# Output chunks of the second layer follow their slices by 2.1 slots instead of 2.2

## The chip, the cores and the metric

The kernel runs on one core of one Trainium2 chip. The metric is the device time of one launch in microseconds (us), median of three runs: 1363.01 before the change (1361.18 to 1366.76). TensorE (PE in the profile) multiplies, VectorE (DVE) and ScalarE (ACT) work on tiles element by element, GpSimd (POOL) does some subtractions and issues the loads of weights, SyncE (SP) issues the other transfers. Each engine works through its own list in order, and waits for the others by semaphores.

## The reference

Attention with 32 landmarks per head gives `x` of 4608 tokens by 512. A first layer without bias follows, `h = ((x @ w1) * (x @ w2)) @ w3 @ w_out`, again 4608 by 512. The second layer, which the change touches, is

```python
def _moe2_ref(x, w_in, w_out):          # x 4608x512, w_in 512x2048, w_out 2048x512
    h = x @ w_in
    g = np.where(h > 0.0, h, np.exp(np.minimum(h, 0.0)) - 1.0)
    return g @ w_out
```

All in float32. The kernel reaches that accuracy by splitting each operand into a high and a low part and adding three products (high by high, high by low, low by high).

## The kernel before

Attention and the first layer take the first 612 us and are not touched. The second layer takes the rest.

**Blocks, slices, slots.** The 4608 tokens are cut into five blocks of 768, 1024, 1024, 1024 and 768 (`BLOCKS`, L31). The 2048 hidden columns are cut into eight slices of 256 (`NPAIR`). One block with one slice is one unit `u`, numbered 0 to 39: block `u // 8`, slice `p = u % 8`. The program goes through 41 *slots*; slot `u` holds the first multiplication of unit `u`, and the later work of the units before it. What stands in a slot, and in which order, is written out by hand in `SLOTS` (L126), by the kind of slot: "narrow" for blocks of 768, "mid" for blocks of 1024, "first" and "last" for the first and the last slice of a block.

**A step** (`h0` to `h6`, `step`, L940) is one of the seven products of a Strassen-like scheme for `x @ w_in`: six matmuls on PE (L925 to L927) into one of four PSUM banks (`hat`, `hmm`). DVE adds each bank to its partners (L956) or ACT copies it (L950); then the bank is free for the step four further on.

**The ELU** of unit `u` begins in slot `u` (`R`, `E`: ACT, L972 to L977) and ends in slot `u + 1` (`s`: DVE L981; `a`: DVE L985 and ACT L990, which gives the high part `eh`; `l`: DVE L996, the low part `el`).

**A chunk** (`oo`, L1015) is the product of 128 tokens of a unit with its 256 rows of `w_out`: six matmuls (L1031 to L1033) that read `eh`, `el` and the weights `wo` of that unit. Chunks of two units share a bank of their own (`oa`): for a pair of units U, U+1 (U even) the list `work` has four rows of chunks, first half of the tokens by U, first half by U+1 (which ends the sums), second half by U, second half by U+1. A row has four chunks in a block of 1024 and three in a block of 768. So a pair has 16 or 12 chunks, called chunk 0, 1, 2, ... here. Each has a due time, and at each `c` in a slot all chunks that are due by then are put in, as one *burst* on PE:

```python
            for k, (a, d) in enumerate(((0, 0), (0, 1), (1, 0), (1, 1))):
                t = u + (FIRST if u + k == 0 else LAG)
                work += [(t + (k * nch + c) / (2 * nch), u + d, a * nch + c) for c in range(nch)]

        def chunks(t):
            n = sum(x[0] <= t + 1e-6 for x in work)
```

A "mid" slot has one burst, after `h6`. A "narrow" and a "first" slot have one after `h3` and one after `h6`.

**What a chunk brings with it.** When a sum is ended, `evict` (L1041) adds the bank to the output tile (DVE, L1009; ACT copies it, L1007, for the first two slices of a block) and stores it. It is called after each step and ahead of each chunk that starts a sum. And the last chunk of a unit issues the load of the weights of the unit two further on into the buffer that it has just read:

```python
            if c == 2 * nch - 1:
                wo2.pop(u)
                if u + 2 < n2 - 2:
                    load_wo(u + 2)
```

There are two such buffers (`wo`, 1 MB a load, L861), and two for the weights of the steps (`wh`, 1.75 MB a load, L852). Both are loaded from POOL's queue, as are POOL's subtractions `tv` for the next block (L891, in the slots of slices 3 to 6). POOL's queue is in order: a load whose buffer is still read holds up what stands behind it. `wh` of unit `u + 1` is issued at the start of slot `u`.

Of the kernel before, what the change touches and what calls it, by code (L numbers as in the profile page):

```python
# [120 lines left out]
"""  # L121


LAG = 2.2
FIRST = 1.9
SLOTS = {  # L126
# [12 lines left out]
def nystrom_moe_kernel(ctx, tc, qT, kT, vm, vr, w12, w3T, w_out1, w_in2, w_out2, out):  # L139
# [490 lines left out]
    with tc.manual_schedule():  # L630
# [419 lines left out]
        for u in range(0, n2, 2):  # L1050
            nch = BLOCKS[units2[u][0]][1] // 256
            for k, (a, d) in enumerate(((0, 0), (0, 1), (1, 0), (1, 1))):
                if u == n2 - 2:
                    a, d = d, a
                t = u + (FIRST if u + k == 0 else LAG)
                work += [(t + (k * nch + c) / (2 * nch), u + d, a * nch + c) for c in range(nch)]
# [112 lines left out]
```

## Time and profile before

| | |
|---|---|
| median of three runs | 1363.01 us |
| the profiled execution's own time | 1363.48 us |
| its span, first to last instruction | 1361.7 us |
| PE busy | 1333.0 us (98%) |
| DVE, ACT, POOL busy | 968.5 (71%), 681.1 (50%), 331.1 us (24%) |
| mean granted clock of PE | 0.998 |

The span is what the profile shows; some 1.8 us of the time lie around it. A matmul's row has a modelled end: matmuls are pipelined, and the next one begins before the row of the one before has ended. So how long PE stood is read from the starts of its rows, and the idle time in brackets is a little less than that. "PEld" is PE's loading of weights into the array, which runs beside the matmuls.

### The profile page before, as it was taken

To read this page: it belongs to the slowest core of one execution; us is meant where nothing else is said; L and a number is where in the kernel's file an instruction comes from. 1 tells how busy PE (TensorE), PEld (TensorE's weight loads), DVE (VectorE), ACT (ScalarE), POOL (GpSimd) and SP (SyncE) were. 2 spreads that over 40 slices of the span, in tenths; PEclk is the share of its full clock that TensorE was granted. 3 is DMA by queue.
4 is the path that set the end of the run, shared out by engine and by line. 5 is a ranking of instruction groups with operands and counts; after the bars stand their busy time and mean duration, and the time that the engine had idled before them with its cause. 6 is when DMAs were issued, how large, how long until landed. Compare 5 with 4: busy or idle time off the path is not lost.

```text
span 1361.7 us, 23607 instructions
## 1 busy us (share of the span) xinstructions
PE 1333.0 (98%) x9504; PEld 1115.1 (82%) x9504; DVE 968.5 (71%) x1628; ACT 681.1 (50%) x1189; POOL 331.1 (24%) x327
## 2 busy tenths in 40 slices
PE   5999999999999999999999999999999999999998
PEld 2458888988888888999988788887888878888897
DVE  7988767776787667447787667975768746786575
ACT  6665444454545354446565444555355454453442
POOL 5544342532562523301200121001110020100000
PEclk9999999999999999999999999999999999999999
DMA  8865436546565343417545544363443633446541
GB/s 344 316 210 175 155 131 220 207 142 214 180 210 181 110 163 119 166 60 293 203 171 182 209 170 170 116 233 116 169 170 120 235 135 128 170 174 239 181 156 46
DMA packets 61326, 241.38 MB, mean 177 GB/s; under 512 B 5409, under 2 KB 14625, under 8 KB 53025
## 3 DMA queue, kind: packets, MB, share of 16 engines
q1 hardware_dynamic: 44576, 124.53, 26.0%
q0 software_dynamic: 16640, 115.35, 23.6%
q8 instruction: 74, 1.21, 0.4%
q14 instruction: 36, 0.29, 0.1%
HBM read 197.92 MB, written 41.94 MB: 176 GB/s over the span
## 4 chain that ended last, share of the span: by engine, by line
PE 91%; DMA 6%; DVE 1%; issue 1%; ACT 0%; POOL 0%; SPq 0%; DVEq 0%; POOLq 0%; ACTq 0%
PE oa L1031 8%; PE oa L1033 8%; PE oa L1032 8%; PE ab L782 6%; PE y L818 5%; PE y L819 5%; PE ab L783 5%; PE y L820 5%; PE ab L784 5%; DMA wo<-wo_d 4%; PE hat L927 4%; PE hat L926 4%; PE hat L925 4%; PE hmm L925 4%; PE hmm L927 4%; PE hmm L926 4%
## 5 line engine op out<-in xcount | busy, mean ns | idle before, releaser
L1031 PE MATMUL oa<-wo,eh 128*128 128x512 f32 x552 | 216.7, 393 | 7.4 <-DMA wo<-wo_d 7.4
L1033 PE MATMUL oa<-wo,el 128*128 128x512 f32 x552 | 216.7, 392 | 0.0
L1032 PE MATMUL oa<-wo,eh 128*128 128x512 f32 x552 | 216.5, 392 | 0.0
L981 DVE SCALAR_TENSOR_TENSOR t<-m,t 128x1024 f32<-128x1024 f32 (+1 forms) x80 | 102.4, 1280 | 106.3 <-ACT m L977 106.2
L972 ACT ACTIVATE m<-g 128x1024 f32<-128x1024 f32 (+1 forms) x80 | 75.7, 968 | 204.4 <-DVE g L956 204.4
L782 PE MATMUL ab<-ath,mh 128*128 128x288 f32 x512 | 157.7, 308 | 1.3 <-DVE g L796 1.2
L861 POOL DMA_DIRECT2D wo<-wo_d x38 | 27.4, 721 | 535.3 <-PE oa L1033 532.6
L818 PE MATMUL y<-gh,w3oh 128*128 128x288 f32 x512 | 156.0, 305 | 0.0
L819 PE MATMUL y<-gl,w3oh 128*128 128x288 f32 x512 | 151.3, 295 | 0.0
L783 PE MATMUL ab<-atl,mh 128*128 128x288 f32 x512 | 151.2, 295 | 0.0
L820 PE MATMUL y<-gh,w3ol 128*128 128x288 f32 x512 | 151.0, 295 | 0.0
L784 PE MATMUL ab<-ath,ml 128*128 128x288 f32 x512 | 150.5, 294 | 0.0
L1031 PEld LDWEIGHTS oa<-wo,eh 128*128 128x128 f32 x552 | 104.0, 188 | 33.1 <-DMA wo<-wo_d 11.5
L990 ACT CAST eh<-t 128x512 fp32r<-128x512 f32 (+1 forms) x160 | 84.3, 574 | 91.0 <-DVE t L985 91.0
L1033 PEld LDWEIGHTS oa<-wo,el 128*128 128x128 f32 x552 | 104.0, 188 | 22.3 <-DVE el L996 0.2
L1032 PEld LDWEIGHTS oa<-wo,eh 128*128 128x128 f32 x552 | 103.9, 188 | 21.7
L782 PEld LDWEIGHTS ab<-ath,mh 128*128 128x128 f32 x512 | 96.0, 188 | 24.8 <-issue 14.3
L818 PEld LDWEIGHTS y<-gh,w3oh 128*128 128x128 f32 x512 | 96.2, 188 | 18.1 <-issue 16.8
L790 ACT COPY a<-ab 128x288 f32<-128x288 f32 x128 | 51.0, 399 | 108.2 <-PE ab L784 107.7
L927 PE MATMUL hat<-yb,wh 128*128 128x512 f32 (+1 forms) x280 | 103.2, 369 | 0.0
L927 PE MATMUL hmm<-yb,wh 128*128 128x512 f32 (+1 forms) x280 | 103.2, 368 | 0.0
L925 PE MATMUL hmm<-yb,wh 128*128 128x512 f32 (+1 forms) x280 | 103.1, 368 | 0.1
(173 smaller groups left out, 3052.5 us busy)
## 6 DMA issues: line engine op xcount, KB each, us to landing
wh<-wh_d POOLq DMA_DIRECT2D x40, 1792.0 KB, 8.9
wo<-wo_d POOLq DMA_DIRECT2D x38, 1024.0 KB, 5.3
wo_raw<-in_w_out_dram SPq DMA_DIRECT2D x24, 512.0 KB, 5.8
q<-in_qT_dram SPq DMA_DIRECT2D x8, 1152.0 KB, 6.5
k<-in_kT_dram SPq DMA_DIRECT2D x8, 1152.0 KB, 6.7
out_dram<-o SPq DMA_DIRECT2D x36, 256.0 KB, 2.3
yd<-ysb SPq DMA_DIRECT2D x15, 576.0 KB, 3.6
w_raw<-in_w3T_dram SPq DMA_DIRECT2D x16, 512.0 KB, 5.8
```

The costliest lines, as they stand in the source:

```text
L782: pe.matmul(p[:, :NH], mh[:, cs], ah[:, blk, :], start=(blk == 0), stop=False)
L783: pe.matmul(p[:, :NH], mh[:, cs], al[:, blk, :], start=False, stop=False)
L784: pe.matmul(p[:, :NH], ml[:, cs], ah[:, blk, :], start=False, stop=(blk == 1))
L818: pe.matmul(a[oc][:, :NH], w3o_hi[fc][:, os_], gh, start=(fc == 0), stop=False)
L819: pe.matmul(a[oc][:, :NH], w3o_hi[fc][:, os_], gl, start=False, stop=False)
L820: pe.matmul(a[oc][:, :NH], w3o_lo[fc][:, os_], gh, start=False, stop=(fc == K1 - 1))
L925: pe.matmul(o, ah, bh[:, kk, :], start=(kk == 0), stop=False)
L926: pe.matmul(o, ah, bl[:, kk, :], start=False, stop=False)
L927: pe.matmul(o, al, bh[:, kk, :], start=False, stop=(kk == 1))
L1031: pe.matmul(oacc[c], eh[:, ts_], w[:, 0, :], start=start and j == 0, stop=False)
L1032: pe.matmul(oacc[c], eh[:, ts_], w[:, 1, :], start=False, stop=False)
L1033: pe.matmul(oacc[c], el[:, ts_], w[:, 0, :], start=False, stop=stop and j == 1)
```

## The change

One number. The due time of a chunk, counted in slots, becomes 0.1 less for all pairs and rows but the very first row, which has its own constant.

```diff
-LAG = 2.2
+LAG = 2.1
```

In the blocks of 1024 the chunks of a pair are due 1/8 slot apart: at U + 2.2, 2.325, ... 3.95, 4.075 before, so the sixteenth (chunk 15) falls into the burst of slot U + 4; at U + 2.1, ... 3.85, 3.975 now, so it falls into the burst of slot U + 3. In the blocks of 768 they are 1/6 slot apart, and the same holds for the twelfth (chunk 11), which was due at U + 4.033 and is now due at U + 3.933. A middle row shifts in the same way: the last chunk of the second row moves from the burst of slot U + 3 to that of slot U + 2.

**PE, end of slot 12** (block 1). `hmm` is the bank of the last step, `wo_9` and `wo_10` the weights of units 9 and 10, the `oa` are the banks of the chunks. Before:

```order
L927 MATMUL hmm_8548<-yb_9610,wh_9985 128x512
L1031 MATMUL oa_10107<-wo_9_9931,eh_9844 128x512
L1032 MATMUL oa_10107<-wo_9_9931,eh_9844 128x512
L1033 MATMUL oa_10107<-wo_9_9931,el_9845 128x512
L1031 MATMUL oa_10107<-wo_9_9931,eh_9872 128x512
L1032 MATMUL oa_10107<-wo_9_9931,eh_9872 128x512
L1033 MATMUL oa_10107<-wo_9_9931,el_9873 128x512
L1031 MATMUL oa_10237<-wo_10_10114,eh_9994 128x512
```

Now the same place:

```order
L925 MATMUL hmm_8548<-yb_9619,wh_9991 128x512
L926 MATMUL hmm_8548<-yb_9620,wh_9991 128x512
L927 MATMUL hmm_8548<-yb_9619,wh_9991 128x512
L1031 MATMUL oa_10237<-wo_10_10114,eh_10000 128x512
L1032 MATMUL oa_10237<-wo_10_10114,eh_10000 128x512
L1033 MATMUL oa_10237<-wo_10_10114,el_10001 128x512
```

The six matmuls of chunk 15 that read `wo_9` now stand seven steps earlier, at the end of slot 11; the burst of slot 12 begins with chunk 0 of the next pair.

**POOL, slots 11 to 13.** Loads and subtractions in the order of the queue; `wo_11` is the load that the chunk shown above issues.

```order
 L861 DMA wo_10_10114<-wo_d 128x2x1024
-L852 DMA wh_10138<-wh_d 128x3584
-L891 TENSOR_TENSOR tv_9988<-yin_9835,tv_9987 128x1024
-L861 DMA wo_11_10234<-wo_d 128x2x1024
-L852 DMA wh_10287<-wh_d 128x3584
-L891 TENSOR_TENSOR tv_9989<-yin_9835 128x1024
+L861 DMA wo_11_10140<-wo_d 128x2x1024
+L852 DMA wh_10146<-wh_d 128x3584
+L891 TENSOR_TENSOR tv_9994<-yin_9843,tv_9993 128x1024
+L852 DMA wh_10293<-wh_d 128x3584
+L891 TENSOR_TENSOR tv_9995<-yin_9843 128x1024
```

The load of the odd unit's weights goes ahead of one load of `wh` and one subtraction; the two loads of `wo` of a pair now stand together.

**DVE, start of a slot in block 1.** L981 is the second `s`, L1009 the evictions, L956 the first sum of the steps. Before:

```order
L981 SCALAR_TENSOR_TENSOR t_10370<-m_10369,t_10370 128x1024
L1009 TENSOR_TENSOR o_10158<-oa_10382,o_10158 128x512
L1009 TENSOR_TENSOR o_10158<-oa_10389,o_10158 128x512
L1009 TENSOR_TENSOR o_10161<-oa_10396,o_10161 128x512
L956 TENSOR_TENSOR s_10463<-hmm_8549,s_10452 128x512
```

Now:

```order
L981 SCALAR_TENSOR_TENSOR t_10377<-m_10376,t_10377 128x1024
L1009 TENSOR_TENSOR o_10166<-oa_10382,o_10166 128x512
L1009 TENSOR_TENSOR o_10166<-oa_10389,o_10166 128x512
L1009 TENSOR_TENSOR o_10169<-oa_10396,o_10169 128x512
L1009 TENSOR_TENSOR o_10169<-oa_10403,o_10169 128x512
L956 TENSOR_TENSOR s_10472<-hmm_8549,s_10460 128x512
```

The fourth eviction of a row, which before stood behind the sums of this slot's last step, now stands with the other three ahead of the first sum.

## Rows read from the trace of the kernel before

**Rows 1.** The page: share of the chain that ended last, by engine.

```profile
PE 91%; DMA 6%; DVE 1%; issue 1%; ACT 0%; POOL 0%; SPq 0%; DVEq 0%; POOLq 0%; ACTq 0%
```

**Rows 2.** Waits of PE and PEld, 612 to 1362 us: total us, times, longest.

```profile
PE oa L1031 <- DMA wo<-wo_d: 7.4, 10, 2.7
...
PEld hmm L925 <- DVE g L956: 0.4, 1, 0.4
PEld oa L1031 <- ACT o L1007: 0.4, 1, 0.4
```

**Rows 3.** Timeline of PE, slots 18 and 19: start, us, instruction, [idle before <- who].

```profile
922.10 0.39 PE L1031 MATMUL oa<-wo,eh 128*128 128x512 f32 x1
...
928.72 0.39 PE L1033 MATMUL oa<-wo,el 128*128 128x512 f32 x1
930.28 0.50 PE L1031 MATMUL oa<-wo,eh 128*128 128x512 f32 x1 [1.17 <-DMA wo<-wo_d]
930.61 0.40 PE L1032 MATMUL oa<-wo,eh 128*128 128x512 f32 x1
...
934.49 0.40 PE L925 MATMUL hat<-yb,wh 128*128 128x512 f32 x1
```

**Rows 4.** Timeline of PE, burst of slot 17: its first matmul, and what follows it.

```profile
901.60 0.39 PE L1031 MATMUL oa<-wo,eh 128*128 128x512 f32 x1
...
912.52 0.40 PE L925 MATMUL hmm<-yb,wh 128*128 128x512 f32 x1
```

**Rows 5.** Timeline of PE, second burst of slot 34.

```profile
1254.20 0.34 PE L927 MATMUL hat<-yb,wh 128*128 128x384 f32 x1
1257.19 0.64 PE L1031 MATMUL oa<-wo,eh 128*128 128x512 f32 x1 [2.65 <-DMA wo<-wo_d]
...
1261.63 0.34 PE L925 MATMUL hat<-yb,wh 128*128 128x384 f32 x1
```

**Rows 6.** Windows around that burst: stretch, us, busy by engine, granted clock, DMA, GB/s.

```profile
1257.00:1258.00 1.00, 0.81 (x2) 0.67 (x3) 0.97 (x2) 0.97 (x2) 0.00 (x0) 0.70 0.87 287
1258.00:1260.00 2.00, 2.00 (x6) 1.56 (x5) 1.46 (x2) 1.97 (x4) 0.00 (x0) 0.50 1.00 416
1260.00:1262.00 2.00, 2.00 (x9) 1.64 (x9) 0.19 (x1) 0.01 (x1) 0.00 (x0) 0.80 0.60 244
```

**Rows 7.** Timeline of POOL: burst of slot 12, and two slots of block 4.

```profile
799.87 0.74 POOL L861 DMA_DIRECT2D wo<-wo_d  x1 [11.33 <-PE oa L1033]
800.61 0.55 POOL L852 DMA_DIRECT2D wh<-wh_d  x1
...
1290.42 0.56 POOL L852 DMA_DIRECT2D wh<-wh_d  x1 [6.51 <-PE hmm L927]
...
1305.97 0.56 POOL L852 DMA_DIRECT2D wh<-wh_d  x1 [2.44 <-PE hat L927]
```

**Rows 8.** The loads of `wo`, and those of `wh`, after 612 us: from issue to landing.

```profile
DMA to landing us min/median/max: 5.2/5.3/9.8
DMA to landing us min/median/max: 7.1/8.9/14.5
```

**Rows 9.** Timeline of DVE and PE: a sum that frees a bank, the matmul that takes it.

```profile
897.18 0.68 DVE L956 TENSOR_TENSOR g<-hat,s 128x512 f32<-128x512 f32 x1
...
900.23 0.39 PE L925 MATMUL hat<-yb,wh 128*128 128x512 f32 x1
...
752.71 0.68 DVE L956 TENSOR_TENSOR g<-hat,s 128x512 f32<-128x512 f32 x1
...
754.56 0.39 PE L925 MATMUL hat<-yb,wh 128*128 128x512 f32 x1
```

**Rows 10.** Timeline of POOL and DVE in the burst of slot 11, and DVE in slot 18.

```profile
786.13 2.41 POOL L891 TENSOR_TENSOR tv<-yin,tv 128x1024 f32<-128x1024 f32 x1
786.20 3.42 DVE L981 SCALAR_TENSOR_TENSOR t<-m,t 128x1024 f32<-128x1024 f32 x1
...
916.17 1.22 DVE L985 TENSOR_TENSOR t<-t,g 128x1024 f32<-128x1024 f32 x1
```

## The prediction

> **What bounds the kernel now.** I read the page's chain first: 91% of it is PE and 6% is DMA [rows 1]. So PE sets the end, and a change of order can only give back time in which PE stands, or make it stand more. The waits of PE in the second layer come next. There is one kind of any weight: chunk matmuls that wait for the load of `wo`, 7.4 us in 10 waits, the longest 2.7 [rows 2]. PEld's waits for other engines are two of 0.4 us [rows 2]. The third view is PE's timeline at those waits. All ten stand in even slots: 10, 12, 14, 18, 20, 22, 26, 28, 30 in the blocks of 1024, and 34 in the last block. In slot 18 the burst begins at 922.10, and at 928.72 + 0.23, after five chunks, PE stops until 930.28 [rows 3]. The sixth chunk (chunk 4 of the new pair) is the first of the odd unit and needs that unit's weights. POOL's timeline says why they are late: in slot 12 the load is issued at 799.87, right when chunk 15 of the pair before has been done, since it fills the buffer that chunk 15 has read [rows 7]. It lands 5.3 us later by the median [rows 8], and four chunks of six matmuls at 0.23 are 5.5 us, so 0.74 of issue and anything on the DMA engines beside it shows as a stall.
>
> **The stalls that go.** With the change chunk 15 is the last of slot U + 3, and the load is issued there, a whole run of seven steps and four chunks ahead of its first use. What the ten stalls cost, step by step:
> - The idle time itself: 7.4 us [rows 2].
> - What the rows hide. A matmul's row is 0.39 long, but the next one starts after 0.23 (a burst of 48 matmuls without a stall takes 10.92, [rows 4]); the idle time counts from the modelled end, so each stall loses 0.16 more: 10 x 0.16 = 1.6 us.
> - The first matmul after a stall holds up the next by 0.33 and not 0.23 (930.28 to 930.61) [rows 3]: nine times 0.10 = 0.9 us.
> - The clock. After the longest stall, in slot 34 (nothing between 1254.20 and 1257.19), the granted clock is 0.70, 0.50 and 0.80 in three windows of 1, 2 and 2 us [rows 5, 6]. That is 2.4 GHz falling to 1.2 and coming back; it loses 0.3 + 1.0 + 0.4 = 1.7 us. The two chunks there take 1261.63 - 1257.19 = 4.44 us, where 12 matmuls at 0.23 are 2.8: the same 1.7. The stall of slot 18, with 1.17 of idle, does not show slower matmuls after the first one.
>
> Sum 11.6 us. As a control: the eight chunks of slot 18 take 934.49 - 922.10 = 12.39 us, those of slot 17, without a stall, 912.52 - 901.60 = 10.92 [rows 3, 4]; the difference is 1.47, the terms give 1.17 + 0.16 + 0.10 = 1.43.
>
> The two small waits of PEld, 0.4 us each [rows 2], go as I read the order. The one on ACT is a chunk that takes a bank whose sum was ended first in the same burst (block 0); that sum now ends a slot earlier. The one on DVE is in slot 7, where one more chunk now stands ahead of the first step and DVE gets 1.4 us more. I count half of their 0.8, so 12.0 us in all.
>
> **What is moved, and what hides it.**
> - The matmuls of the moved chunks: their number and size stay. What they read (`eh`, `el`) was already needed by the chunks next to them in the earlier burst. Cost 0.
> - The loads of `wo` of the odd units: POOL now waits for the end of chunk 15 before it can issue the `wh` that is needed one slot later, and the `tv` behind it. Before, `wh` and `tv` waited for chunk 11. So `wh` leaves four chunks, 5.5 us, later in a block of 1024. Cover: it used to land 7.1 to 14.5 us after issue [rows 8], and the pattern "one `wo` 0.74 us ahead of it" is what rows 7 show, so its median of 8.9 holds this already. In a block of 768 a slot is 1305.97 - 1290.42 = 15.55 us [rows 7]; issue at slot start + 0.7 (one `wo` issue) and landing 8.9 to 14.5 later is 9.6 to 15.2. That just fits. Bounds of the cost: 0, and if the second `wo` delayed the slowest landing by its own whole 5.3 us [rows 8], 15.2 + 5.3 - 15.55 = 5 us in each of the eight pairs of narrow slots, 40 us. I take 0, since the median row is far inside. A gain is excluded: PE waits for no `wh` in rows 2.
> - The loads of `wo` of the even units go one chunk earlier or stay. Cost 0.
> - The fourth eviction. DVE now does four adds, and not three, ahead of the first sum of a slot, some 0.68 us more (a 128x512 instruction of DVE, [rows 9]), and none later in that slot. Who waits: the bank of the third step, freed by a sum that ends at 897.86, is taken at 900.23, so 2.4 us are to spare; the tightest place that I found in a block of 1024 is slot 10, 753.39 against 754.56, 1.2 us [rows 9]. Both are over 0.68. In the narrow slots one more chunk now stands ahead of the first step, 1.4 us that DVE gets. Bounds: 0 to 0.68 in each slot where the spare time were gone; I take 0. The `evict` inside the burst goes away; DVE had no wait of PE on it there.
> - POOL's `tv` of slices 4 and 6. Before, it ran in the burst: at 786.13 for 2.41 us, and a DVE instruction that began at 786.20 took 3.42, where the same size takes 1.22 [rows 10]. So the two hold each other up, by 2.2 us here. Now `tv` starts some 1.5 us into the slot (after the issue of `wo` and `wh`, 0.74 + 0.55, [rows 7]) and runs to about 3.9. DVE's first instruction on two tiles of SBUF starts at 916.17 in a slot that begins at 912.52, 3.65 in [rows 4, 10]: a collision of 0.3 us, against 2.4 to spare. I take 0; bounds 0 to the full 2.2.
>
> The Trainium skill (SBUF — State Buffer, section "Who interferes with whom") has a rule that speaks against the change here: a VectorE instruction with two SBUF inputs and a GpSimd instruction that reads SBUF exclude each other for a whole instruction, and the first to start wins. Rows 10 agree (3.42 against 1.22). By the rule alone, with the collision at its worst in each of the eight slots, the sum would be that of the first rival below; by the place of the row at 916.17 it is 12.0.
>
> **Sum.** The profiled execution took 1363.48 us, span 1361.7. 1363.48 - 12.0 = 1351.5. The median of the runs is 1363.01, 0.47 less, so 1351.0 us for the median.
>
> **The rivals.**
> 1. DVE eats the spare time. The fourth add (0.68) and a full collision with `tv` (2.2) make 2.9, against 2.4 to spare: PE waits 0.5 us in each of the eight slots of slices 4 and 6, and if the wait comes at two banks, 1.0: 4 to 8 us back. For it: rows 10 show such a collision. Against it: that one, in the slot before, cost PE nothing in rows 2, and the new place is mostly free of instructions on two tiles. Time 1351.0 + 4 = 1355.
> 2. The stalls only change their name. If ACT and DVE, and not the load, were what paces a slot (relu of one slot to first chunk of the next), PE would meet them as soon as the load is early, and the time stays at 1363. For it: the two small waits of PEld [rows 2] show that DVE and ACT come close to PE at two places. Against it: the load can only show as last if all else was ready by then, and between the stalled slots PE runs bursts of 10.92 without any wait [rows 4]. That the change does not do what it says is excluded by the order of POOL.
> 3. Slower: `wh` comes late in the narrow slots. One mechanism: POOL's queue holds `wh` back until the last chunk of the pair, and the two loads of `wo` in front of it keep the DMA engines. It decides from a landing of 14.8 us after issue (15.55 - 0.74). At the far bound of 5 us in eight slots the time is 1351 + 40 = 1391, and each such stall would be longer than the one of slot 34 and bring its 1.7 us of half clock: 1405. For it: 14.5 has been seen [rows 8]. Against it: that is the longest of all, and the median, 8.9, is 6 us inside the limit. The change is slower than before by over 0.5% from a landing 2.4 us later than that in all eight slots.
>
> **How the numbers follow.** The forecast has 0.80, with a range of its own of 1349 to 1353.5 (the 0.8 of PEld, half a stall left, and 1.5 us of spread as the three runs show it). Rival 1 has 0.09, rival 2 has 0.08, rival 3 has 0.03. About 0.5%, 6.8 us, is what a measurement of this kernel can tell from no change, so faster means under 1356.2. The forecast and two thirds of rival 1 lie there, 0.86; rival 2 and the rest of rival 1 make 0.11 the same; rival 3 makes 0.03 slower. The range is 1348.5 to 1357: it leaves out rivals 2 and 3 and the end of rival 1, and at its low end has the runs' own spread.
>
> **What would show it.** In the profile after, PE's waits for `wo` in the second layer are gone (10 to 0, at most one), bursts of eight chunks all take 10.9 us, and the granted clock has no dip near 1257. POOL's timeline has two `wo` issues some 6 us apart and `wh` right behind. The first layer ends at 612 as before. It would be wrong if PE waits for `wh` (rival 3), for DVE at a bank of the steps (rival 1), or if PE's row of waits is empty and the time has not moved (rival 2).

## The result, and the profile after

| | before | after |
|---|---|---|
| median, runs made together | 1363.69 us (1361.18 to 1366.76) | 1350.68 us (1349.41 to 1351.77) |
| profiled execution, its span | 1363.48, 1361.7 us | 1351.77, 1350.0 us |
| PE busy | 1333.0 us | 1327.9 us |
| mean granted clock of PE | 0.998 | 0.999 |

The ratio is 0.9903, with a 95% interval of 0.988 to 0.9926: faster by some 1%. 1351.0 us was forecast. The chain of the page, which answers to [rows 1], has lost its DMA part:

```profile
PE 93%; DVE 1%; ACT 0%; POOL 0%; issue 0%; DVEq 0%
```

The waits of PE and PEld in the second layer (total us, times, longest), which answer to [rows 2]:

```profile
PE oa L1031 <- ACT o L1007: 0.5, 1, 0.5
...
PEld oa L1031 <- ACT o L1007: 0.9, 1, 0.9
PEld oa L1033 <- DVE el L996: 0.2, 1, 0.2
```

No wait for `wo` is left, of ten. The wait of PEld for the sum `g` of DVE is gone too; the short one for `el` in the last row stood there before as well. The wait for ACT is not gone: it has grown, and PE itself now waits there. That is the one thing that the prediction had the wrong way round.

PE's timeline of slot 18 after (start, us, instruction) answers to [rows 3]:

```profile
921.66 0.39 PE L1031 MATMUL oa<-wo,eh 128*128 128x512 f32 x1
...
932.58 0.40 PE L925 MATMUL hat<-yb,wh 128*128 128x512 f32 x1
```

From first chunk to next step it is 932.58 - 921.66 = 10.92 us, what a burst without a stall took before [rows 4], against 12.39. All 20 bursts of eight chunks take 10.92 us now. POOL's timeline, which answers to [rows 7], shows why:

```profile
784.01 0.74 POOL L861 DMA_DIRECT2D wo<-wo_d  x1 [23.01 <-PE oa L1033]
789.45 0.72 POOL L861 DMA_DIRECT2D wo<-wo_d  x1 [4.70 <-PE oa L1033]
790.17 0.57 POOL L852 DMA_DIRECT2D wh<-wh_d  x1
790.74 2.41 POOL L891 TENSOR_TENSOR tv<-yin,tv 128x1024 f32<-128x1024 f32 x1
```

The two loads of `wo` of a pair stand 5.4 us apart at the end of slot 11, and `wh` right behind the second. Before, this second load was issued at 799.87, in the burst that needed it. What the loads take has hardly changed; from issue to landing, `wo` and then `wh`, as in [rows 8]:

```profile
DMA to landing us min/median/max: 5.2/5.3/9.5
```

```profile
DMA to landing us min/median/max: 7.5/8.8/12.6
```

Where slot 34 had its dip [rows 6], the windows after (columns as there) show full clock:

```profile
1248.00:1250.00 2.00, 2.00 (x10) 1.63 (x10) 0.48 (x1) 1.97 (x3) 0.16 (x1) 1.00 1.10 402
1250.00:1252.00 2.00, 2.00 (x12) 1.76 (x11) 1.43 (x2) 1.94 (x4) 0.00 (x0) 1.00 1.15 449
```

**Where the time came from.** From the first chunk to the start of the last matmul the second layer took 1357.30 - 622.22 = 735.08 us before and 1345.57 - 622.45 = 723.12 after: 11.96 less. I took the starts of all its matmuls, and what each interval has over a regular one (0.228 us, 0.174 for 384 columns). The ten stalls, the slow matmuls behind them and the half clock cost 11.7 before, and all of it is gone; the wait for DVE in slot 7 gave 0.35; the wait for ACT in slot 3 cost 0.22 before and costs 0.77 now. That makes 11.7 + 0.35 - 0.55 = 11.5; the remaining 0.46 is spread over some 3300 regular intervals, and no run shows its cause.

**The wait that grew.** In slot 3 (block 0), DVE, POOL, ACT and PE after:

```profile
633.96 2.40 POOL L891 TENSOR_TENSOR tv<-yin 128x1024 f32<-128x1024 f32 x1 [3.25 <-DMA yin<-yd]
635.30 1.87 DVE L981 SCALAR_TENSOR_TENSOR t<-m,t 128x768 f32<-128x768 f32 x1 [2.21 <-ACT m L977]
...
638.25 0.93 ACT L990 CAST eh<-t 128x384 fp32r<-128x384 f32 x2 [0.49 <-PE hat L927]
639.08 0.47 ACT L950 COPY s<-hat 128x384 f32<-128x384 f32 x1
639.45 1.56 ACT L1007 COPY o<-oa 128x512 f32<-128x512 f32 x3
...
639.21 0.40 PE L1033 MATMUL oa<-wo,el 128*128 128x512 f32 x1
640.10 0.50 PE L1031 MATMUL oa<-wo,eh 128*128 128x512 f32 x1 [0.49 <-ACT o L1007]
```

And of before, the same DVE and POOL instructions:

```profile
633.22 2.41 POOL L891 TENSOR_TENSOR tv<-yin 128x1024 f32<-128x1024 f32 x1 [2.74 <-DMA yin<-yd]
...
635.08 1.36 DVE L981 SCALAR_TENSOR_TENSOR t<-m,t 128x768 f32<-128x768 f32 x1 [2.21 <-ACT m L977]
```

`tv` and `s` overlap in both, and in both `s` ends 0.81 us after `tv`, as if it had waited for it. After, `tv` runs until 636.36, over more of `s`, which takes 1.87 us and not 1.36 (0.96 without a collision, as the second `s` of that slot shows). ACT's casts need the max that DVE makes behind `s`, which ends at 638.16. (The row of the casts names `hat` for their wait; when the same kernel was run again, that row named DVE.) ACT's three evictions follow the casts, so the chunk at 640.10 finds its bank still occupied. The rule in the Trainium skill that the prediction weighed (SBUF — State Buffer, "Who interferes with whom") holds here as in [rows 10]; the prediction counted it for the blocks of 1024 alone, and it came through in a narrow one.

Whether the change itself moved `tv` towards `s` is not shown. `tv` waits for a transfer, and begins 1.86 us ahead of `s` in the one profile of before, but 0.75 to 1.5 us ahead in the profiles of after and of the nine runs below that have `tv` in this slot, also in those that move only half of the chunks.

### The profile page after: what moved, and what is told of

Read it like the earlier page. It is cut to its first block, busy times and chain, and to the rows that moved or that the text cites. A ratio compares the mean times of both kernels' runs of the same rounds, so it can differ in the third digit from the quotient of the medians.

```text
span 1350.0 us, 23602 instructions
## 1 busy us (share of the span) xinstructions
PE 1327.9 (98%) x9504; PEld 1114.7 (83%) x9504; DVE 958.8 (71%) x1628; ACT 681.3 (50%) x1189; POOL 330.5 (24%) x327
## 4 chain that ended last, share of the span: by engine, by line
PE 93%; DVE 1%; ACT 0%; POOL 0%; issue 0%; DVEq 0%
PE oa L1033 10%; PE oa L1032 10%; PE oa L1031 9%; PE ab L782 6%; PE y L818 6%; PE y L819 5%; PE y L820 5%; PE ab L783 5%; PE ab L784 5%; PE hat L927 4%; PE hmm L927 4%; PE hat L926 4%; PE hmm L926 4%; PE hat L925 4%; PE hmm L925 4%; PE m L375 2%
## 5 line engine op out<-in xcount | busy, mean ns | idle before, releaser
L981 DVE SCALAR_TENSOR_TENSOR t<-m,t 128x1024 f32<-128x1024 f32 (+1 forms) x80 | 91.1, 1139 | 115.6 <-ACT m L977 115.6
L796 DVE TENSOR_TENSOR g<-ab,a 128x288 f32<-128x288 f32 x128 | 57.8, 451 | 64.6 <-PE ab L784 32.5
L927 PE MATMUL hmm<-yb,wh 128*128 128x512 f32 (+1 forms) x280 | 103.2, 368 | 0.0
```

The lines of the kernel that those rows point to most:

```text
L927: pe.matmul(o, al, bh[:, kk, :], start=False, stop=(kk == 1))
```

## The experiments

All ratios are to the kernel before, run on the same chip. The edits are to the kernel after. The theory: the whole gain is the earlier load of the odd units' `wo`. Its rivals: the order of the chunks and evictions has a part in it, and DVE's spare time, `tv` or `wh` is near its limit, so that some of the gain was eaten.

### One row of chunks or the other

The change acts on the rows of both units of a pair. With 0.1 less for the last two rows alone (the last chunk, and with it the load):

```diff
-                t = u + (FIRST if u + k == 0 else LAG)
+                t = u + (FIRST if u + k == 0 else LAG if k > 1 else 2.2)
```

> Due times 0.1 earlier only for the third and fourth row of a pair (the last chunk of a pair moves, and with it the load); the second row stays at 2.2, so its last chunk stays in the burst of slot U + 3, with bursts of 7 and 9 chunks. Theory A: the whole gain, 1349.5 to 1353, no wait for wo. Theory B (rows that end with the slot matter in themselves): 1355 to 1360.

1352.02 us, ratio 0.9912 (0.9895 to 0.9928); no wait for `wo`. With 0.1 less for the first two rows alone (`LAG if k < 2 else 2.2`):

> The opposite: 0.1 earlier only for the first and second row, so the chunk in the middle moves and the last chunk of a pair, with its load, stays in the burst of the next pair. Theory A: no gain, ten waits for wo as before, 1361 to 1366. Theory B: 1355 to 1359.

1363.98 us, ratio 0.9998 (0.9988 to 1.0007). PE's waits for `wo` there:

```profile
PE oa L1031 <- DMA wo<-wo_d: 6.1, 9, 2.6
```

So the half that moves the last chunk holds the whole gain, and the other half nothing. This one does not yet part the load from the chunk that issues it.

### The load alone, put back

Now all chunks stay where the change put them, and only the load of the odd unit is held until the next even slot: POOL copies one column of the last sum of that slot's steps, and issues the load behind that. The load of `wh` and the `tv` that the change put behind this load on POOL's queue go ahead of it again; PE waits for no `wh` in these kernels.

```diff
+        pend, last = [], []
...
                 dve.tensor_tensor(d, o, sq[x], op=ALU.add)
+                last[:] = [d]
...
+        def flush(src):
+            while pend:
+                w = p2r.tile([128, 1], F32, name=f"late{pend[0]}", tag="late")
+                pool.tensor_copy(w, src)
+                load_wo(pend.pop(0))
...
+            if pend and u % 2 == 0 and c == 0:
+                flush(last[0][:, :1])
...
-                    load_wo(u + 2)
+                    if u % 2:
+                        pend.append(u + 2)
+                    else:
+                        load_wo(u + 2)
```

> The chunks stand as in the changed kernel (all by 2.1), but the load of an odd unit's wo is issued only when the burst of the next even slot begins, about where it was issued before the change. POOL is held there by a copy of one column of the last sum that DVE has made. Theory A (the whole gain is the earlier load): PE waits for wo again, 9 to 11 times, 6 to 11 us in all, and the time is 1360 to 1365, as before the change. Theory B (a good part of the gain is the order of chunks and evictions, which stays): 1352 to 1357.

1379.58 us, ratio 1.0104 (1.0075 to 1.0132): a miss. The stalls came back, but larger than in the kernel before. Waits of PE for `wo`, and POOL's timeline in slot 12:

```profile
PE oa L1041 <- DMA wo<-wo_d: 20.6, 14, 2.4
```

```profile
804.22 0.18 POOL L1020 COPY late<-g 128x1 f32<-128x1 f32 x1 [12.18 <-DVE g L957]
804.70 0.75 POOL L861 DMA_DIRECT2D wo<-wo_d  x1 [0.30 <-issue]
```

I had overlooked that the burst no longer begins with chunk 15. The first chunk that needs the load is the fifth of the burst and not the sixth, 1.37 us earlier (six matmuls at 0.228). In the kernel before the load of slot 12 was issued at 799.87 for a matmul that would have started at 804.86, 4.99 us later; here at 804.70 for one that would have started at 808.31, 3.61 us later. So PE waits 13.2 us more than before (20.6 against 7.4, in fourteen stalls and not ten), and the clock falls three times and not once, at some 1.55 us each in the starts of the matmuls. That is some 16 us; the overshoot is 15.1 (1379.58 against 1364.51 for before on that chip). The next kernel takes the lost lead back: the hold ends with an earlier sum.

```diff
-                last[:] = [d]
+                last[:] = [d] if k < 5 else last
```

> The kernel after, with the odd units' loads of wo held back as in the first of these experiments, but by an earlier sum (s of step 4, which ends some 1.2 us before the last one), so that the load is issued about 0.6 us into the burst and has about 4.9 us until its first use, where the kernel before gave it about 5.4. Theory A (the place of the load is the whole effect, and the overshoot of the first of these experiments came from 1.4 us less lead): PE waits for wo return as 10 to 14 waits of 0.3 to 1.5 us, 8 to 13 us in sum, at most two dips of the clock, time 1362 to 1370, ratio to before 0.999 to 1.005. Theory B (the hold itself, the POOL copy on DVE's sum and the wh behind it, costs time apart from the lead): time stays over 1374.

1363.27 us, ratio 1.0004 (0.9987 to 1.002): the time of the kernel before. Its waits for `wo`, and the load:

```profile
PE oa L1041 <- DMA wo<-wo_d: 10.5, 14, 1.7
```

```profile
801.78 0.18 POOL L1020 COPY late<-s 128x1 f32<-128x1 f32 x1 [10.99 <-DVE s L957]
802.26 0.74 POOL L861 DMA_DIRECT2D wo<-wo_d  x1 [0.30 <-issue]
```

The load now stands 4.81 us ahead of its first use (807.07 without the stall), 1.2 us more than in the kernel above. Only the nine stalls in the blocks of 1024 shrink by it, from 16.3 to 6.8 us of waiting; the five in the narrow blocks stay about as they were. In all, PE waits 10.1 us less, and the three falls of the clock are gone: with 1.55 us each, 14.8 of the 15.1 us by which the two second layers differ (750.57 and 735.46 us from the first chunk to the start of the last matmul).

So with the chunks and evictions in the order of after, and only the load about where it was, the gain is gone. That fits the theory. That it is the time of before so exactly is in part luck: the 14 stalls cost 14.5 us here, where the ten of before cost 11.7, and the regular intervals take 2.2 us less than in after, for which no run shows a cause. More delay costs more: here the load waits, in the blocks of 1024, for the second relu of that even slot (`kinds[0]` is the kind of the slot; narrow and first slots keep the hold of the first of these kernels):

```diff
+                    if t == "R0" and kinds[0] not in ("narrow", "first") and u % 2 == 0 and u > 2:
+                        flush(mt[u, 0][0][:, :1])
```

> As e1_late_load, but in the slots with one burst the load waits for the second relu of the slot on ACT, some 2.2 us later still. Theory A: each of the nine stalls in blocks of 1024 (and some more, since every even slot now has one) gets 2 us longer, 12 of them, so 25 to 40 us over the changed kernel, 1375 to 1392; stalls of 2.6 us of idle or more bring a dip of the granted clock to 0.5 as the one of slot 34 did before, shorter ones do not. Theory B: under 1365, because the order pays part.

1416.11 us, ratio 1.0379 (1.0359 to 1.0398), over the expected range: the clock fell in nine of the stalls, and in eight of them that cost some 2.7 us each, more than the 1.6 of slot 34 before. PE's waits for `wo`:

```profile
PE oa L1041 <- DMA wo<-wo_d: 38.7, 14, 4.1
```

The place of the load alone takes the time from 1351 to 1363, 1380 and 1416 us.

### Was part of the gain eaten?

First `tv`. It goes one slot later, away from slot 3; the kernel after was run again beside it.

```diff
-            if i + 1 < NBL and 3 <= p < 7:
-                sums_y(i + 1, p - 3)
+            if i + 1 < NBL and 4 <= p < 8:
+                sums_y(i + 1, p - 4)
```

> On the changed kernel, POOL's subtractions tv run in the slots of slices 4 to 7 and no longer 3 to 6, so none stands beside the first ELU instruction of slot 3. Theory: the one wait that is left in the second layer (slot 3, ACT evicts a bank 0.75 us late) comes from tv, which holds up DVE's first instruction there (1.87 us for 0.96), and through it ACT. Then PE's waits in the second layer are empty, 0.5 to 0.8 us less than the changed kernel. Rival: it comes from the third eviction that now stands in ACT's queue ahead; then the wait stays at 0.5 or more and the time is the same.

> The changed kernel once more, as the mark for the three runs beside it: 1349 to 1352.

1353.51 us (ratio 0.9919, 0.9904 to 0.9934) against 1352.31 of the kernel after (0.9907, 0.9893 to 0.9922; 0.3 us over what was expected). PE has no wait left in the second layer, and DVE's row in slot 3 is short:

```profile
636.39 0.96 DVE L981 SCALAR_TENSOR_TENSOR t<-m,t 128x768 f32<-128x768 f32 x1 [2.21 <-ACT m L977]
```

So the collision was the cause of the wait that grew. Its price, 0.8 us, is too small for the runs: the intervals overlap.

Then DVE's spare time: in blocks 1 to 3 the last max of the second half of the ELU is done once more, 1.2 us of DVE in each of 24 slots, without effect on the values.

```diff
-            dve.tensor_tensor(t, t, h_tile(u, j), op=ALU.max)
+            for _ in range(2 if j and 8 <= u < 32 else 1):
+                dve.tensor_tensor(t, t, h_tile(u, j), op=ALU.max)
```

> On the changed kernel, DVE does the maximum of the ELU of the second half twice in the units of the blocks of 1024 (the result is the same): 1.2 us more in each of 24 slots, ahead of the sum that frees the third step's bank. The prediction counted 2.4 us to spare there before, and 0.68 less at the most after the fourth eviction. Theory: over 1.2 us is left, the time stays within 1 us of the changed kernel, with no wait of PE for DVE in blocks 1 to 3 but perhaps in slot 10. Rival (the first one of the prediction, DVE has eaten the spare time): PE waits 0.4 to 1 us in most of the 24, 10 to 24 us more.

1352.46 us, ratio 0.9911 (0.9897 to 0.9926), with one short wait for DVE (the row below, 0.7 us in slot 10). With `range(4 ...)`, 3.6 us a slot:

> As e4a with three more, 3.6 us in each of 24 slots. If 2.4 us are to spare, PE waits some 1.2 us in each: 25 to 35 us more than the changed kernel. If 1.7 (less 0.68), 1.9 in each: 40 to 50 us. If DVE were far from PE's path, under 5 us.

1415.35 us, ratio 1.0367 (1.0346 to 1.0388), more than either bound. The waits of PE for DVE's sums, with one more max and with three:

```profile
PE hat L925 <- DVE g L956: 0.7, 1, 0.7
```

```profile
PE hat L925 <- DVE g L956: 26.0, 12, 3.7
PE hmm L925 <- DVE g L956: 8.6, 6, 1.9
PE hmm L925 <- DVE s L956: 5.8, 3, 2.0
```

DVE has over 1.2 us to spare in nearly all slots of these blocks, and less than 3.6 in each. The one slot with a wait is 10, the tightest that the prediction had found, with 1.2 us to spare before [rows 9]. There one more eviction (the third, as its row comes from a narrow block) did not take room away. After, the sum ends at 754.86 and its bank is taken at 756.19, which is 1.3 us to spare, as DVE now begins this slot 0.86 us ahead of PE's first step (0.12 before):

```profile
754.18 0.68 DVE L956 TENSOR_TENSOR g<-hat,s 128x512 f32<-128x512 f32 x1
756.19 0.39 PE L925 MATMUL hat<-yb,wh 128*128 128x512 f32 x1
```

With the max once more, DVE's first instruction of the slot begins 0.8 us later against PE's first step, and the max itself takes 1.2: these 2.0 us against 1.3 make the wait of 0.7. As PE waits for DVE nowhere in the kernel after, the added evictions are covered everywhere. Three more maxes, at 63 us over the kernel after, miss all three expectations: the clock falls eight times there, at 1.4 to 1.6 us each, some 12 us that they had not counted.

Last `wh`: a spare copy of 1 MB, which nothing reads, goes ahead of it on POOL's queue in the even slots from slot 4 on.

```diff
+                if u % 2 == 0 and u > 2:
+                    pool.dma_start(out=spare, in_=wo_d[0:2].rearrange("f p a n -> p f a n"))
                 load_wh(max(u, 1) + 1)
```

> The kernel after, with a spare 1 MB copy from DRAM to DRAM on POOL's queue ahead of wh in the even slots from 4 on (nothing reads it), so that wh stands behind the last chunk, the load of wo and 1 MB more. It asks how much room wh has. Theory A (room of some us in the blocks of 1024, and 1 to 3 us in those of 768): wh lands 13 to 18 us after its issue in those slots, no wait of PE in blocks 1 to 3; in blocks 0 and 4, with slots of 15.5 us, up to seven waits of 0 to 3 us, and a few with a dip of the clock: 1351 to 1370. Rival 3 of the prediction (wh was already near its limit, and the loads ahead of it delay it by their whole time): waits for wh in most of the 18 even slots, 3 to 8 us each, over 1400.

1352.88 us, ratio 0.9923 (0.9895 to 0.9951). The landing of `wh`, and PE's one wait for it, at the first step of slot 35 (L926 there is L925 of the other kernels):

```profile
DMA to landing us min/median/max: 7.6/10.7/15.1
```

```profile
1250.56 0.39 PE L1034 MATMUL oa<-wo,el 128*128 128x512 f32 x1
1252.17 0.45 PE L926 MATMUL hat<-yb,wh 128*128 128x384 f32 x1 [1.23 <-DMA wh<-wh_d]
```

With another megabyte ahead of it `wh` is late once, by 1.2 us, at 15.1 us of landing. Up to seven waits were expected. The prediction's limit for a narrow slot was 14.8 us from issue to landing; here PE would have gone on at 1250.79, 13.8 us after the issue at 1237.01. The kernel after has its slowest load of `wh` at the same place. It lands 12.56 us after its issue, at 1249.85, and PE begins to use it at 1251.26:

```profile
1237.28 0.56 POOL L852 DMA_DIRECT2D wh<-wh_d  x1
1251.26 0.34 PE L925 MATMUL hat<-yb,wh 128*128 128x384 f32 x1
```

So the change left 1.4 us to spare in slot 34, where the same load had 13.7 before. That is the nearest that the third rival came.

## Why the prediction was right, point by point

- **The stalls.** Ten waits for `wo` were to go: they went. Idle time, hidden starts, slow matmuls and half clock were put at 11.6; 11.7 came. The load, put back without the chunks, takes the gain away (1363.27), and the chunks moved without the load give none (1363.98): shown.
- **The two small waits of PEld.** This step failed, by a size that no run can tell. Half of 0.8 was to go. The wait for DVE went (0.35); the one for ACT was read as "that sum now ends a slot earlier", but what it waits for is ACT, which still comes to the eviction late, and later than before by the collision with `tv`. It cost 0.55 more. The net is 0.2 lost instead of 0.4 gained. Moving `tv` shows that the wait comes from the collision. The prediction also counted two such waits of PEld; a third, of 0.2 us for `el`, stands in both kernels.
- **`tv` at the start of the slot.** Costed 0, as an overlap of 0.3 us in the blocks of 1024. There the collision came much as costed, at five places, with 0.2 to 0.4 us (the row below, where `tv` runs until 793.15, takes 1.62 us and not 1.22), and no wait of PE with it. That rows 10 show the two holding each other up was too much said: `tv` took its usual 2.41 there, and only DVE lost. In block 0 the subtraction waits for the data of the next block, and so ran into `s`; the prediction had not looked at that block.

```profile
792.63 1.62 DVE L985 TENSOR_TENSOR t<-t,g 128x1024 f32<-128x1024 f32 x1
```

- **The fourth eviction** (0): right; PE waits for DVE nowhere, and one max more is still nearly free.
- **`wh` later by four chunks** (0): right, but nearer than it was made. It lands in 12.6 us at most, and stands a further megabyte nearly everywhere. The step "issue at slot start + 0.7" was short for slot 34: POOL gets the end of the last chunk only 0.86 us into the slot (1235.71 to 1236.57), so `wh` is issued 1.57 in, and 1.4 us were left, not 6.
- **The moved chunks and the earlier loads of even units** (0): nothing is seen of them.
- **The rivals.** DVE at its limit is refuted by one more max that cost nothing measurable; stalls that change their name, by the empty waits and bursts of 10.92; a late `wh`, by the further megabyte.
- **From the sum to the median**: 1363.48 - 12.0 was 1351.5 for a profiled execution; the profiled one took 1351.77. That 12.0 meets the 11.96 of the second layer so closely is in part luck: 0.1 more from the stalls and 0.46 from regular intervals, which nobody had counted, make up for the 0.6 of the small waits.

## What to carry to other kernels

When a matmul waits for a load, look at which instruction frees the load's buffer: moving that instruction across the boundary of a stage gained 12 us here without any work saved, and the gain could be counted beforehand from idle time, hidden starts, the slow first matmul and the clock. An experiment that puts such a load back must keep its distance to the first use, not its place in the program; here 1.2 us of distance in nine stalls, with the falls of the clock that came with it, made the difference between 1363 and 1380. What moves the load may also delay what stands behind it in the queue: ask where that has least room left, as `wh` in slot 34. Where PE hardly waits, removing what still collides (`tv`) is not seen in the time.

## What the runs showed of the hardware

**The length of a stall does not settle whether the clock falls.** In the kernel with the load held back, PE stood twice in the same place of a slot. At 767.26, 2.46 us after the start of the matmul before it, the clock stayed; at 853.07, after 2.24 us, it fell one microsecond later. The two starts in PE's timeline, and the windows behind them (us, busy by engine, granted clock, DMA, GB/s):

```profile
764.80 0.39 PE L1043 MATMUL oa<-wo,el 128*128 128x512 f32 x1
767.26 0.50 PE L1041 MATMUL oa<-wo,eh 128*128 128x512 f32 x1 [2.07 <-DMA wo<-wo_d]
...
850.82 0.39 PE L1043 MATMUL oa<-wo,el 128*128 128x512 f32 x1
853.07 0.50 PE L1041 MATMUL oa<-wo,eh 128*128 128x512 f32 x1 [1.86 <-DMA wo<-wo_d]
```

```profile
767.00:769.00 2.00, 1.74 (x8) 1.43 (x9) 2.00 (x2) 1.43 (x3) 0.00 (x0) 1.00 1.10 459
...
854.00:856.00 2.00, 2.00 (x7) 1.57 (x6) 0.69 (x1) 1.14 (x2) 0.00 (x0) 0.54 1.05 437
856.00:858.00 2.00, 2.00 (x7) 1.53 (x7) 0.30 (x1) 0.00 (x0) 0.00 (x0) 0.61 0.30 119
```

Before, the stall of slot 34 with its 2.65 us of idle time was the only one with a fall from 2.4 to 1.2 GHz [rows 5, 6], and I had expected shorter ones to bring none. The longest in the kernel at 1363.27 (2.11 from start to start) brought none: the profiled run has a mean clock of 1.0 there, against 0.998 before. In the kernel at 1416 all nine of 4.0 to 4.5 us brought one. After eight of them PE came back at half clock at once, as in the second row. After the longest, of 4.52, it came back at full clock at 771.84, and the clock fell some 0.8 us later, in the window of the first row:

```profile
772.00:773.00 1.00, 1.00 (x4) 0.82 (x5) 1.00 (x2) 0.40 (x1) 0.00 (x0) 0.83 1.07 444
...
866.00:867.00 1.00, 0.88 (x2) 0.79 (x3) 0.00 (x0) 0.41 (x1) 0.00 (x0) 0.50 1.07 444
```

Nor does a kernel's own order settle it: of four executions of the kernel with the load held back, three had a mean clock of 0.995 or 0.996 and took 1379 to 1381 us, and one had 0.999 and took 1372.6. What decides between the two stalls near 2.3 us stays open.

**A copy's time from issue to landing is not what it costs the load behind it.** The spare copy of the last experiment takes 7.5 us from issue to landing by the median:

```profile
DMA to landing us min/median/max: 7.3/7.5/10.9
```

The `wh` issued right behind it lands 11.3 us after its issue by the median of these slots, against 9.0 in the kernel after: only 2.3 us later, where 13 to 18 us had been expected. The trace's record of the packets shows why. In slot 4 `wo`, the copy and `wh` are issued at 650.18, 650.90 and 651.49, and land at 655.4, 658.4 and 662.4. The copy's 256 packets start between 654.84 and 657.41, and the first packet of `wh` at 657.31. So the three transfers of this queue follow one another, and most of the copy's 7.5 us is the start of a transfer and its waiting for the load ahead; its packets take some 2.6 us.
